# Query and key rows through device memory, value sums two iterations behind, and another order inside the score batches, in a fused attention and feed-forward block

## The chip, the cores and the metric

The kernel runs on one core of a Trainium2 chip. The metric is the device time of one execution in microseconds; lower is better. TensorE (PE) does the matmuls, ScalarE (ACT), VectorE (DVE) and GpSimd (POOL) the work on elements, and the queue of SyncE (SP) issues most transfers; ACT's queue issues some, between its own instructions.

## The reference

A transformer block with adaptive layer norm on S = 2048 tokens of D = 640, one batch, in fp32: 32 heads of 20, a causal window of 256, a feed-forward width of 1536.

```python
mod = (silu(c) @ w_mod).reshape(1, 6, 1, -1)
sa, ca, ga, sb, cb, gb = (mod[:, i] for i in range(6))
h = layernorm(x) * (1 + ca) + sa
q, k, v = (h @ wqkv) as (heads, tokens, 20) each
scores = q @ k.T * 20 ** -0.5
p = softmax(where(0 <= i - j < 256, scores, -1e9))
x = x + ga * ((p @ v) @ wo)
h = layernorm(x) * (1 + cb) + sb
x = x + gb * (gelu(h @ w1 + b1) @ w2 + b2)
```

## The kernel before

Matmuls of fp32 operands are made of three products of a high and a low part each (hi by hi, lo by hi, hi by lo). The program runs in stages: the modulation and the first projections; a loop over attention, into which the other projections are woven; the rest of the attention output and its projection; and the feed-forward part.

**The loop.** The sequence is two halves of 1024 tokens. A quad is four heads, and there are 8 quads in a half; a block is 128 tokens, 8 in a half. An iteration t takes one (half, quad, block), 128 in all. It holds, in this order on PE:

- the scores s of item t (keys by queries, for the row maximum), and the scores e of the item LAG = 11 earlier (for the exponential). s and e are one *score batch*: four heads each, two on the upper and two on the lower rows of the PE array, in two or three PSUM banks. The matmuls of a batch are six kinds: a the upper rows' part in the bank that both row halves share, b and c the upper rows' in their own banks, d and e the lower rows' own, f the lower rows' shared part. The order is the table ONE (one batch) or BOTH (e is batch 0, s batch 1). [...]
- the value sums o of a query block whose last exponential came PVLAG = 1 iteration earlier (pv_stage), which ACT copies to oT (pv_copy) ahead of the exponential of e to pt (e_exp). In between DVE masks e, and POOL cuts a triangle off pt (affine_select).
- the work that a plan has put there for (t, 0..3): projection units of 15 matmuls (pp), layer norm steps, weight loads, modulation.

Every eighth iteration PE transposes the row maxima of the last quad, ACT copies them to mt (m_rows), and four transfers on ACT's queue put them as rows 60, 61, 124 and 125 into that quad's two query buffers (m_store), so that e comes out with the maximum subtracted. e reads them three iterations later.

**Rows.** A unit of q or k makes 128 features of 512 tokens. ACT writes the high part, POOL or DVE the low part into a stage tile, one buffer for q and one for k with both unit halves of 1024 tokens (tags stage0, stage1). When the second is finished (build), its rows are cut by head and put on a list; flush issues from it two to four pieces in an iteration on SP's queue, two transfers each, into the query and key buffers qbuf and kbuf. They hold two heads each (a pair: head e on partitions from 64e, 60 rows: hi, copy of hi, lo), NBUF = 9 of each. The key buffers' last 256 columns of the first half are carried to the second by k_scr in device memory. Until the pieces have landed, ACT may not write the next unit into the stage tile.

**What sets the order.** Each engine's queue runs in order, and the code is recorded in the order in which it stands (Ordered, line 112: the profile names every instruction by that line). UNITS is the order of the units, which a planner places by due times into iterations. Transfers of SP and ACT together take eight semaphores in turn; a transfer waits until the one eight before it has landed, if that is not known already, and an engine that issues it stands meanwhile. The prediction's names: pp is the projection bank, pf its copy by ACT for POOL, stage the stage tile, hhi and hlo the normed input, whi and wlo the weights, wraw a weight as loaded, nm the negative maximum, xt an input tile, o_scr the sums in device memory.

Of the kernel before, what the change touches and what calls it, by code (L numbers as in the profile page):

```python
# [17 lines left out]
P = 128  # L18
# [10 lines left out]
NBUF = 9  # L29
NVB = 5  # L30
LAG = 11
PVLAG = 1
# [22 lines left out]
ONE = "0a 0e 0b 0d 0c 0f".split()  # L55
BOTH = "0a 0e 0b 0d 1a 1e 0c 0f 1d 1b 1c 1f".split()
# [10 lines left out]
FL = 4  # L67
# [50 lines left out]
def block_kernel(ctx: ExitStack, tc: tile.TileContext, x, wqkv, wo, w1, b1, w2, b2, c, crow, wmod, wcol, sel, outT):  # L118
# [12 lines left out]
    k_scr = scratch("k_scr", [NP, 124, 256])  # L131
# [242 lines left out]

    qb_ = [att.tile([P, HALF], F32R, name=f"qbuf{i}") for i in range(NBUF)]
    kb_ = [att.tile([P, 256 + HALF], F32R, name=f"kbuf{i}") for i in range(NBUF)]
# [3 lines left out]
    def ones_k(bufs):  # L380
        for i in bufs:
            for e in range(2):
                nc.sync.dma_start(
                    f32(kb_[i][64 * e + 60 : 64 * e + 64, :]).rearrange("p (r n) -> p r n", n=P),
                    ones[0:4, None, :].to_broadcast([4, (256 + HALF) // P, P]),
                )


    def qbuf(half, pair):
        return qb_[(half * NP + pair) % NBUF]  # L390

    def kbuf(half, pair):
        return kb_[(half * NP + pair) % NBUF]

# [5 lines left out]
    stage = {}  # L400
    quads = {}
    early = [nc.sync]
    clock = [0]
    now = [0]
    pending = []
    done_pairs = set()
    done_v = set()
    last_v = {}
    built = {(0, 0): 4 * DH, (0, 1): 4 * DH}

    def ready(half, pair):
        n = half * NP + pair - NBUF
        return n < 0 or n in done_pairs

    def build(half, kind, j):
        parts = stage.pop((half, kind, j))
        f = j * P
        while f < (j + 1) * P:
            h, d0 = divmod(f, DH)
            n = min(DH - d0, (j + 1) * P - f)  # L420
            if half or h >= 4:
                pending.append((half, kind, h, d0, n, f - j * P, parts, clock[0]))
            f += n

    def flush(limit=2):
        for _ in range(limit):
            able = [p for p in pending if ready(p[0], p[2] // 2) and p[-1] < clock[0]]
            if not able:
                return
            urgent = [p for p in able if 8 * (p[0] * QUADS + p[2] // 4) <= now[0] + 8]  # L430
            piece = urgent[0] if urgent else able[0]
            pending.remove(piece)
            half, kind, h, d0, n, r0, parts, _ = piece
            pair = h // 2
            dst, off = (qbuf(half, pair), 0) if kind == 0 else (kbuf(half, pair), 256)
            if half == 1 and (half, pair) not in built:
                nc.sync.dma_start(f32(kbuf(half, pair)[0:124, 0:256]), k_scr[pair])

            r = 64 * (h % 2)
            src = f32(parts[r0 : r0 + n])  # L440
            two = src if kind == 0 else src[:, 0:1].to_broadcast([n, 2, HALF])
            eng = early[0] if kind else nc.sync
            eng.dma_start(f32(dst[r + 2 * d0 : r + 2 * (d0 + n), off : off + HALF]), two)
            nc.sync.dma_start(f32(dst[r + 40 + d0 : r + 40 + d0 + n, off : off + HALF]), src[:, kind])
            built[half, pair] = built.get((half, pair), 0) + n

    def unit(half, kind, j, c2, eng, acc=None):
# [18 lines left out]
        def qk_hi():  # L466
            if c2 == 0:
                assert not [1 for e in pending if e[1] == kind], key
                stage[key] = prj.tile([P, 2, HALF], F32R, tag=f"stage{kind}", name=f"stage{half}_{kind}_{j}")
            nc.scalar.mul(stage[key][:, 0, cs], box["ps"], sc)  # L470
# [6 lines left out]
        def qk_lo():  # L477
            hi, lo = stage[key][:, 0, cs], stage[key][:, 1, cs]
# [4 lines left out]
            if c2 == 1:  # L483
                build(half, kind, j)
# [103 lines left out]
    def s_batch(it):  # L588
        half, quad, qb, g = it["key"]
        if qb == 0:  # L590
            it["quad"]["nm"] = att.tile([P, 4, NQB], F32, tag="nm", bufs=2, name=f"nm{half}_{quad}")
        t, s = score_banks("s", f"s{half}_{quad}_{qb}")
        c0 = 384 - P * min(g + 1, 3)
        parts = []
        for h in HEADS:
            pair, r = 2 * quad + h // 2, slice(64 * (h % 2), 64 * (h % 2) + 60)
            assert built.get((half, pair)) == 4 * DH, (half, pair, built.get((half, pair)))
# [71 lines left out]
    def e_exp(it, e):  # L669
        half, quad, i = it["key"]  # L670
        pt = att.tile([P, 4, 384], F32, tag="pt", bufs=4, name=f"pt{half}_{quad}_{i}")
# [270 lines left out]
    flat = [prj.tile([P, 2, D], F32, tag=f"stage{i}", name=f"wc{i}") for i in range(2)]  # L942
    flat.append(vcar.rearrange("p q b v -> p (q b v)")[:, 0 : 2 * D].rearrange("p (g d) -> p g d", d=D))
    wc = [[t[:, g] for g in range(2)] for t in flat]
# [11 lines left out]
    for b in range(0, 4, 2):  # L956
        xt = att.tile([P, 2, D], F32, tag="pt", bufs=4, name=f"xs1_{b}")
# [6 lines left out]
    sel_t = kb_[NBUF - 1]  # L964
    sel_raw = att.tile([P, 8 * P], F32, tag="pt", bufs=4, name="sel_raw")
    nc.sync.dma_start(sel_raw, sel)
    ones_k(range(4))
# [80 lines left out]
    first = {}  # L1048

    def lay_out(c2, kind):  # L1050

        if c2 == 0:
            first[kind] = stage[0, kind, 0]
        cs = slice(c2 * CHUNK, (c2 + 1) * CHUNK)
        for pair in range(2):
# [10 lines left out]
            matmul(ps, sel_t[:, at : at + P], first[kind][:, 0, cs], start=True, stop=False)  # L1066
            matmul(ps, sel_t[:, at + P : at + 2 * P], first[kind][:, 1, cs], start=False, stop=True)
# [44 lines left out]
    ones_k(range(4, NBUF - 1))  # L1112
# [10 lines left out]
    plan = {(0, 1): [lambda: lay_out(1, 0)], (0, 2): [lambda: lay_out(1, 1), lambda: ones_k((NBUF - 1,))]}  # L1123
# [57 lines left out]
    for i, key, c2, pieces, ev in where:  # L1181
# [47 lines left out]
    def to_mid():  # L1229
        assert not pending  # L1230
        prj_ctx.close()
        open_mid()
# [43 lines left out]
    for t in range(n + LAG + PVLAG + 4):  # L1276
        clock[0] += 1
# [38 lines left out]
        if ei:  # L1316
            half, quad, i = ei["key"]
            if i == NQB - 1:
                done_pairs.update((half * NP + 2 * quad, half * NP + 2 * quad + 1))
        if si and si["key"][2] == NQB - 1:  # L1320
            half, quad = si["key"][:2]
            if half == 0:
                for pair in (2 * quad, 2 * quad + 1):
                    nc.sync.dma_start(k_scr[pair], f32(kbuf(0, pair)[0:124, HALF : HALF + 256]))
        flush(3 if t < 12 else FL if t > 100 else 3 if len(pending) > 8 else 2)
        if t == 8:
            early[0] = nc.sync
    assert not pending and not plan
# [121 lines left out]
```

## Time and profile before

| | |
|---|---|
| median of the runs | 1078.03 us (1077.12 to 1083.52, 3 runs) |
| profiled execution, its own time | 1079.06 us |
| its span (first to last instruction) | 1077.0 us |
| PE busy | 990.3 us, 92% |
| 0 to 104 us | modulation, first projections, first iterations |
| 104 to 550 us | loop with projections |
| 550 to 675 us | loop and output projection without the projections of q, k, v |
| 675 to 1077 us | feed-forward part |

A row of the timeline gives start, length, engine, operation with output and inputs, their shapes, the number of like instructions drawn together, and in brackets the idle time just before on that engine and what ended it. A row of the waits gives who waited for whom, the sum in us, how many times, and the longest. Rows of windows are explained where they stand.

### The profile page before, as it was taken

To read this page: it belongs to the slowest core of one execution; us is meant where nothing else is said; L and a number is where in the kernel's file an instruction comes from. 1 tells how busy PE (TensorE), PEld (TensorE's weight loads), DVE (VectorE), ACT (ScalarE), POOL (GpSimd) and SP (SyncE) were. 2 spreads that over 40 slices of the span, in tenths; PEclk is the share of its full clock that TensorE was granted. 3 is DMA by queue.
4 is the path that set the end of the run, shared out by engine and by line. 5 is a ranking of instruction groups with operands and counts; after the bars stand their busy time and mean duration, and the time that the engine had idled before them with its cause. 6 is when DMAs were issued, how large, how long until landed. Compare 5 with 4: busy or idle time off the path is not lost.

```text
span 1077.0 us, 20212 instructions
## 1 busy us (share of the span) xinstructions
PE 990.3 (92%) x7712; PEld 773.7 (72%) x7712; DVE 575.0 (53%) x943; ACT 442.0 (41%) x773; POOL 517.2 (48%) x712
## 2 busy tenths in 40 slices
PE   8989989788898998899978877999999999999998
PEld 7767667566666766667656654888888888888886
DVE  5544867576765686666677654344443324333112
ACT  3633445354644444355443444334343333323222
POOL 4334554466764444454444544376556525642221
PEclk7899999899999999899988887899999999999999
DMA  8156566426144645552451212344341334213213
GB/s 281 39 113 164 127 169 160 114 77 189 54 131 115 165 130 159 159 150 56 110 176 41 61 34 79 107 139 147 118 142 52 112 104 139 61 50 119 89 49 110
DMA packets 81037, 123.60 MB, mean 115 GB/s; under 512 B 9022, under 2 KB 46478, under 8 KB 80942
## 3 DMA queue, kind: packets, MB, share of 16 engines
q1 hardware_dynamic: 69870, 111.95, 36.6%
q10 hardware_dynamic: 10368, 8.92, 2.7%
q0 software_dynamic: 704, 1.44, 0.7%
q8 instruction: 62, 1.02, 0.4%
q14 instruction: 33, 0.27, 0.1%
HBM read 69.74 MB, written 22.15 MB: 85 GB/s over the span
## 4 chain that ended last, share of the span: by engine, by line
PE 70%; ACT 7%; DMA 7%; POOL 5%; DVE 5%; SPq 3%; issue 2%; ACTq 1%; POOLq 0%; DVEq 0%
PE h L112 15%; PE out L112 15%; PE pp L112 13%; PE o L112 6%; PE wo L112 6%; PE e L112 5%; PE s L112 4%; ACT pt L112 4%; SPq L112 3%; POOL pt L112 2%; DVE e L112 2%; DMA qbuf<-stage 2%; DMA o_scr<-oT 1%; DMA qbuf<-mt 1%; ACTq L112 1%
## 5 line engine op out<-in xcount | busy, mean ns | idle before, releaser
L112 POOL TENSOR_SCALAR_AFFINE_SELECT pt<-pt 128x512 f32<-128x512 f32 x192 | 129.6, 675 | 176.7 <-ACT pt L112 170.1
L112 DVE TENSOR_REDUCE nm<-s 128x4 f32<-128x1024 f32 (+1 forms) x128 | 152.6, 1192 | 4.4
L112 POOL TENSOR_TENSOR w2lo<-w2r,w2hi 128x640 fp32r<-128x640 f32 x48 | 75.9, 1582 | 153.9 <-ACT w2hi L112 153.7
L112 PE MATMUL e<-qbuf,kbuf 62*128 62x128 f32 (+2 forms) x792 | 113.8, 341 | 32.6 <-ACT pt L112 32.2
L112 PE MATMUL pp<-hhi,whi 128*128 128x512 f32 x275 | 122.7, 446 | 19.7 <-ACT pf L112 16.5
L112 ACT ACTIVATE pt<-e 128x1024 f32<-128x1024 f32 (+1 forms) x120 | 134.0, 1117 | 16.5 <-DVE e L112 15.9
L112 PEld LDWEIGHTS e<-qbuf,kbuf 62*128 62x128 f32 x792 | 80.6, 200 | 75.9 <-ACT pt L112 52.0
L112 ACT COPY oT<-o 128x128 f32<-128x128 f32 x128 | 34.1, 267 | 228.8 <-PE o L112 190.6
L112 PE MATMUL o<-pt,vbuf 128*32 128x128 f32 x2688 | 111.3, 295 | 8.0 <-POOL pt L112 6.2
L112 DVE CAST ghi<-g 128x512 fp32r<-128x512 f32 x48 | 25.0, 522 | 172.8 <-ACT g L112 172.7
L112 DVE COPY_PREDICATED e<-mask_t,e 128x512 f32<-128x512 uint32 x96 | 66.5, 693 | 94.7 <-PE e L112 90.8
L112 PE MATMUL s<-kbuf,qbuf 60*128 60x256 f32 (+2 forms) x744 | 113.7, 323 | 2.9 <-DVE nm L112 2.3
L112 PE MATMUL pp<-hlo,whi 128*128 128x512 f32 x275 | 114.8, 417 | 0.6 <-POOL hlo L112 0.6
L112 PE MATMUL pp<-hhi,wlo 128*128 128x512 f32 x275 | 114.7, 417 | 0.2 <-POOL wlo L112 0.2
L112 POOL TENSOR_TENSOR wlo<-wraw,whi 128x128 fp32r<-128x128 f32 x185 | 80.4, 465 | 40.9 <-ACT whi L112 33.6
L112 PE MATMUL h<-yhi,w1hi 128*128 128x512 f32 x240 | 96.5, 402 | 0.0
L112 PE MATMUL out<-ghi,w2hi 128*128 128x512 f32 x240 | 96.1, 401 | 0.0
L112 PE MATMUL h<-ylo,w1hi 128*128 128x512 f32 x240 | 94.6, 394 | 0.0
L112 PE MATMUL h<-yhi,w1lo 128*128 128x512 f32 x240 | 94.4, 393 | 0.0
L112 PEld LDWEIGHTS o<-pt,vbuf 128*32 128x32 f32 x2688 | 70.9, 116 | 32.5 <-POOL pt L112 11.2
L112 PE MATMUL out<-ghi,w2lo 128*128 128x512 f32 x240 | 93.8, 391 | 0.0
L112 PE MATMUL out<-glo,w2hi 128*128 128x512 f32 x240 | 93.8, 391 | 0.0
(167 smaller groups left out, 1864.5 us busy)
## 6 DMA issues: line engine op xcount, KB each, us to landing
w2r<-in_w SPq DMA_DIRECT2D x48, 320.0 KB
wraw<-in_wqkv SPq DMA_DIRECT2D x38, 320.0 KB
qbuf<-stage SPq DMA_DIRECT2D x52, 160.0 KB
o_scr<-oT ACTq DMA_DIRECT2D x64, 128.0 KB
kbuf<-stage SPq DMA_DIRECT2D x45, 160.0 KB
wm<-in_wmod SPq DMA_DIRECT2D x20, 320.0 KB
ob<-o_scr SPq DMA_DIRECT2D x16, 320.0 KB
xb<-in_x SPq DMA_DIRECT2D x16, 320.0 KB
```

What stands on the lines that cost most here:

```text
L112: return self.tc.keep_in_program_order(op(*args, **kw))
```

## The change

**Rows.** Stage tiles are 512 tokens of one kind, four buffers under one tag. In the iteration after a unit half is finished, rows_out writes it with two transfers of 128 partitions to q_scr or k_scr in device memory (features by hi, hi, lo by tokens). rows_in reads a quad's four heads back with two transfers of 60 partitions for a kind, into buffers that now hold a quad (NSLOT = 4, each as long as two of the old); it is planned READ = 8 iterations ahead of the quad's first, or two iterations behind the last unit that makes its features where that is later. In the second half the key read takes the 256 columns before it along, so the carry is gone. Rows of a head are interleaved (3d, 3d+1, 3d+2). build, flush and their lists are gone.

**Sums.** PVLAG is 2, and pt has five buffers instead of four.

**Maxima.** The first pair of mt's transfers leaves at the end of the iteration in which it left before, the second an iteration later.

**Order.** ONE and BOTH are new: the parts in the shared banks of both batches stand in the first three places. UNITS of the second half have q and k of the first quads ahead of v.

```diff
-NBUF = 9
+NSLOT = 4
-PVLAG = 1
+PVLAG = 2
-    (1, "q00", "k00", "v00", "q01", "k01", "v01", "q1", "k1", "v1", "q2", "k2", "v20", ...
+    (1, "q00", "k00", "q10", "k10", "q01", "k01", "q11", "k11", "v0", "v1", "q2", "k2", ...
-ONE = "0a 0e 0b 0d 0c 0f".split()
-BOTH = "0a 0e 0b 0d 1a 1e 0c 0f 1d 1b 1c 1f".split()
+ONE = "0a 0d 0b 0e 0c 0f".split()
+BOTH = "0a 0d 1a 0b 0e 0c 1d 1c 0f 1b 1f 1e".split()
...
+    def rows_in(half, quad, kind):
+        i = (half * QUADS + quad) % NSLOT
+        src = qk_scr[kind].rearrange("(Q a e d) l s -> Q e (d l) a s", a=2, e=2, d=DH)[quad]
+        to = qb_[i] if kind == 0 else kb_[i] if half else kb_[i][:, :, 256:]
+        c0 = half * (HALF - 256 * kind)
+        for e in range(2):
+            nc.sync.dma_start(f32(to[64 * e : 64 * e + 60]), src[e][:, :, c0 : c0 + to.shape[2]])
...
-    def flush(limit=2):
...
+    def rows_out():
+        due = [w for w in writes if w[-1] < now[0]]
+        for half, kind, j, c2, st, _ in due:
...
+            nc.sync.dma_start(qk_scr[kind][fs, 0:2, ts], two)
+            nc.sync.dma_start(qk_scr[kind][fs, 2, ts], f32(st[:, kind]))
...
         def qk_hi():
-            if c2 == 0:
-                assert not [1 for e in pending if e[1] == kind], key
-                stage[key] = prj.tile([P, 2, HALF], F32R, tag=f"stage{kind}", ...)
-            nc.scalar.mul(stage[key][:, 0, cs], box["ps"], sc)
+            box["st"] = prj.tile([P, 2, CHUNK], F32R, tag="stage", bufs=4, ...)
+            nc.scalar.mul(box["st"][:, 0], box["ps"], sc)
...
         nc.scalar.copy(mt, ps[0:64])
         it["mt"] = mt
-        m_store(it, 0)
...
+    for half in range(2):
...
+        for quad in range(QUADS):
+            if half or quad:
+                js = range(4 * quad * DH // P, (4 * quad * DH + 4 * DH - 1) // P + 1)
+                due = 8 * (half * QUADS + quad)
+                t = due - READ
+                for kind in range(2):
+                    t = max([t, due - 8 * NSLOT + LAG + 8] + [over_at.get((kind, j), -9) + 2 for j in js])
+                    put(max(t, 0), 3, lambda half=half, quad=quad, kind=kind: rows_in(half, quad, kind))
+                    t += 1
...
+        rows_out()
         for h in range(4):
...
+        for a in range(2):
+            if 8 <= t - a <= n and (t - a) % 8 == 0:
+                m_store(s_items[t - a - 1], a)
         for key in pv_at.get(t, ()):
             pv_store(*key)
-        if turn_m:
-            m_store(s_items[t - 1], 1)
...
-        flush(3 if t < 12 else FL if t > 100 else 3 if len(pending) > 8 else 2)
```

PE, an iteration of the second half in which e of quad 2, block 3 (e1_2_3) and s of quad 3, block 6 (s1_3_6) are made, before; qbuf and kbuf are buffers of one pair, o the value sums:

```order
L112 MATMUL e1_2_3_5639<-qbuf3_96,kbuf3_105 128x256
L112 MATMUL e1_2_3_5639<-qbuf2_95,kbuf2_104 128x128
L112 MATMUL e1_2_3_5639<-qbuf3_96,kbuf3_105 128x128
L112 MATMUL e1_2_3_5639<-qbuf3_96,kbuf3_105 128x384
L112 MATMUL s1_3_6_5640<-kbuf5_107,qbuf5_98 128x256
L112 MATMUL s1_3_6_5640<-kbuf4_106,qbuf4_97 128x128
L112 MATMUL e1_2_3_5639<-qbuf2_95,kbuf2_104 128x384
L112 MATMUL e1_2_3_5639<-qbuf2_95,kbuf2_104 128x256
L112 MATMUL s1_3_6_5640<-kbuf5_107,qbuf5_98 128x384
L112 MATMUL s1_3_6_5640<-kbuf5_107,qbuf5_98 128x128
L112 MATMUL s1_3_6_5640<-kbuf4_106,qbuf4_97 128x384
L112 MATMUL o1_2_1_5656<-pt1_2_0_5503,vcar_116 32x128 x4
```

The same iteration now, where a buffer holds a quad:

```order
L112 MATMUL e1_2_3_5476<-qbuf2_95,kbuf2_99 128x256
L112 MATMUL e1_2_3_5476<-qbuf2_95,kbuf2_99 128x384
L112 MATMUL s1_3_6_5477<-kbuf3_100,qbuf3_96 128x256
L112 MATMUL e1_2_3_5476<-qbuf2_95,kbuf2_99 128x128 x2
L112 MATMUL e1_2_3_5476<-qbuf2_95,kbuf2_99 128x384
L112 MATMUL s1_3_6_5477<-kbuf3_100,qbuf3_96 128x384 x2
L112 MATMUL e1_2_3_5476<-qbuf2_95,kbuf2_99 128x256
L112 MATMUL s1_3_6_5477<-kbuf3_100,qbuf3_96 128x128
L112 MATMUL s1_3_6_5477<-kbuf3_100,qbuf3_96 128x256
L112 MATMUL o1_2_0_5493<-pt1_2_0_5360,vcar_106 32x128 x8
```

e's last matmul was the eighth of twelve and is the ninth; s begins third instead of fifth; the sums are those of block 0 (o1_2_0), where block 1 stood.

ACT, the exchange of the maxima of quad 1 in the second half, before; mt is the transposed maxima, oT the copied sums, pt an exponential, and a name in brackets starting with DMAHW is the semaphore of an earlier transfer:

```order
L112 COPY mt1_1_4860<-pm1_1_4858 64x128 [waits PE_49]
L112 DMA qbuf0_93<-mt1_1_4860 2x8x128 [waits DMAHW4_49,Activation_49]
L112 DMA qbuf0_93<-mt1_1_4860 2x8x128 [waits DMAHW6_49]
L112 DMA o_scr<-oT1_0_1_4778 128x256 [waits DMAHW0_49]
L112 DMA qbuf1_94<-mt1_1_4860 2x8x128 [waits DMAHW2_49]
L112 DMA qbuf1_94<-mt1_1_4860 2x8x128 [waits DMAHW4_49]
L112 COPY oT1_0_2_4905<-o1_0_4_4892 128x128 [waits DMAHW5_49,PE_49]
L112 ACTIVATE pt1_0_6_4907<-e1_0_6_4875 128x4x256 [waits DVE_49,Pool_49]
```

And now:

```order
L112 COPY mt1_1_4737<-pm1_1_4735 64x128 [waits DMAHW4_49,DMAHW5_49,DMAHW1_49,PE_49]
L112 DMA qbuf1_94<-mt1_1_4737 2x8x128 [waits DMAHW6_49,Activation_49]
L112 DMA qbuf1_94<-mt1_1_4737 2x8x128 [waits DMAHW0_49]
L112 COPY oT1_0_1_4718<-o1_0_3_4763 128x128 [waits PE_49]
L112 ACTIVATE pt1_0_6_4777<-e1_0_6_4746 128x4x256 [waits DVE_49,Pool_49]
L112 CAST whi103_4791<-wraw103_4609 128x640 [waits DMAHW5_49]
L112 ACTIVATE stage3_1_2_4799<-pp3_1_2_4728 128x512 [waits PE_49]
L112 ACTIVATE pf3_1_2_4801<-pp3_1_2_4728 128x512 [waits Pool_49]
L112 DMA qbuf1_94<-mt1_1_4737 2x8x128 [waits DMAHW2_49]
L112 DMA qbuf1_94<-mt1_1_4737 2x8x128 [waits DMAHW3_49]
```

Before, the fourth transfer waited on DMAHW4, on which the first had waited too; now the second pair leaves behind the next iteration's exponential and copies, and waits for DMAHW2 and DMAHW3.

SP, around the load of the weight wraw113 and the reading of the denominators rd, before:

```order
L112 DMA kbuf4_106<-stage1_1_2_4801 8x1x1024 [waits DMAHW5_49,Activation_49]
L112 DMA kbuf4_106<-stage1_1_2_4801 4x1024 [waits DMAHW6_49,Pool_49]
L112 DMA kbuf4_106<-stage1_1_2_4801 40x1x1024 [waits DMAHW7_49]
L112 DMA kbuf4_106<-stage1_1_2_4801 20x1024 [waits DMAHW0_49]
L112 DMA kbuf5_107<-stage1_1_2_4801 40x1x1024 [waits DMAHW1_49]
L112 DMA kbuf5_107<-stage1_1_2_4801 20x1024 [waits DMAHW2_49]
L112 DMA r_scr<-rd0_4919 32x4x128 [waits DMAHW4_49,DVE_49]
L112 DMA kbuf5_107<-stage1_1_2_4801 40x1x1024 [waits DMAHW5_49]
L112 DMA kbuf5_107<-stage1_1_2_4801 20x1024 [waits DMAHW6_49]
L112 DMA kbuf7_109<-k_scr 124x256 [waits DMAHW7_49,PE_49]
L112 DMA qbuf7_100<-stage1_0_2_4589 40x1x1024 [waits DMAHW0_49,PE_49]
L112 DMA qbuf7_100<-stage1_0_2_4589 20x1024 [waits DMAHW1_49]
```

And now:

```order
L112 DMA k_scr<-stage2_1_2_4681 128x2x512 [waits DMAHW4_49,Activation_49]
L112 DMA k_scr<-stage2_1_2_4681 128x512 [waits DMAHW5_49,Pool_49]
L112 DMA qbuf3_96<-q_scr 60x2x1024 [waits DMAHW7_49,PE_49]
L112 DMA qbuf3_96<-q_scr 60x2x1024 [waits DMAHW1_49,PE_49]
L112 DMA rd0_4789<-o_scr 128x1x128 [waits DMAHW3_49,DMAHW5_49,DMAHW2_49,DMAHW6_49,DMAHW0_49,Activation_49]
L112 DMA k_scr<-stage3_1_2_4799 128x2x512 [waits Activation_49]
L112 DMA k_scr<-stage3_1_2_4799 128x512 [waits DMAHW7_49,Pool_49]
L112 DMA wraw113_4849<-in_wqkv 128x640
L112 DMA wm5_4_4862<-in_wmod 128x640 [waits DMAHW1_49,DVE_49]
L112 DMA r_scr<-rd0_4789 32x4x128 [waits DVE_49]
L112 DMA kbuf3_100<-k_scr 60x2x1280 [waits DMAHW7_49,DMAHW6_49,DMAHW4_49]
L112 DMA kbuf3_100<-k_scr 60x2x1280 [waits DMAHW5_49]
```

In both stretches a key unit's rows leave the stage tile. Before, they went to the key buffers in pieces; now they go to device memory, two transfers a unit half, and the reads of the quad stand between other rows in the queue and wait for the writes.

More of the change, by code (lines that the diff above doesn't have):

```diff
@@ L373, in w_lo @@
         eng.tensor_tensor(lo[:, kt], raw[:, kt], f32(hi[:, kt]), ALU.subtract)
-    qb_ = [att.tile([P, HALF], F32R, name=f"qbuf{i}") for i in range(NBUF)]
-    kb_ = [att.tile([P, 256 + HALF], F32R, name=f"kbuf{i}") for i in range(NBUF)]
+    qb_ = [att.tile([P, 2, HALF], F32R, name=f"qbuf{i}") for i in range(NSLOT)]
+    kb_ = [att.tile([P, 2, 256 + HALF], F32R, name=f"kbuf{i}") for i in range(NSLOT)]
     vq_ = [att.tile([P, NQB, VQ], F32, name=f"vbuf{i}") for i in range(NVB)]
@@ L383, in ones_k @@
                 nc.sync.dma_start(
-                    f32(kb_[i][64 * e + 60 : 64 * e + 64, :]).rearrange("p (r n) -> p r n", n=P),
-                    ones[0:4, None, :].to_broadcast([4, (256 + HALF) // P, P]),
+                    f32(kb_[i][64 * e + 60 : 64 * e + 64]).rearrange("p a (r n) -> p (a r) n", n=P),
+                    ones[0:4, None, :].to_broadcast([4, 2 * (256 + HALF) // P, P]),
                 )
     def qbuf(half, pair):
-        return qb_[(half * NP + pair) % NBUF]
+        return qb_[(half * QUADS + pair // 2) % NSLOT][:, pair % 2]
     def kbuf(half, pair):
-        return kb_[(half * NP + pair) % NBUF]
+        return kb_[(half * QUADS + pair // 2) % NSLOT][:, pair % 2]
+    def rows_in(half, quad, kind):
[5 more added lines that the diff above has]
+            nc.sync.dma_start(f32(to[64 * e : 64 * e + 60]), src[e][:, :, c0 : c0 + to.shape[2]])
+        if kind:
+            there.add((half, quad))
     def vblk(half, quad, kb):
@@ L398, in vblk @@
         return vq_[(half * QUADS + quad) % NVB][:, kb]
-    stage = {}
+    writes, first = [], {}
+    there = {(0, 0)}
     quads = {}
[L402 to L406, printed above, removed]
+    now = [-1]
     done_v = set()
     last_v = {}
[L409 to L423, printed above, removed]
@@ L425, in flush @@
-    def flush(limit=2):
[L426 to L445, printed above, removed]
+    def rows_out():
+        due = [w for w in writes if w[-1] < now[0]]
+        for half, kind, j, c2, st, _ in due:
+            fs, ts = slice(j * P, (j + 1) * P), slice(half * HALF + c2 * CHUNK, half * HALF + (c2 + 1) * CHUNK)
+            two = f32(st) if kind == 0 else f32(st[:, 0:1]).to_broadcast([P, 2, CHUNK])
+            nc.sync.dma_start(qk_scr[kind][fs, 0:2, ts], two)
+            nc.sync.dma_start(qk_scr[kind][fs, 2, ts], f32(st[:, kind]))
+        del writes[: len(due)]
@@ L466, in qk_hi @@
         def qk_hi():
-            if c2 == 0:
-                assert not [1 for e in pending if e[1] == kind], key
-                stage[key] = prj.tile([P, 2, HALF], F32R, tag=f"stage{kind}", name=f"stage{half}_{kind}_{j}")
-            nc.scalar.mul(stage[key][:, 0, cs], box["ps"], sc)
+            box["st"] = prj.tile([P, 2, CHUNK], F32R, tag="stage", bufs=4, name=f"stage{ch}_{kind}_{j}")
+            nc.scalar.mul(box["st"][:, 0], box["ps"], sc)
         def qk_full():
@@ L482, in qk_lo @@
                 eng.tensor_tensor(lo, box["f"], f32(hi), ALU.subtract)
-            if c2 == 1:
-                build(half, kind, j)
+            writes.append((half, kind, j, c2, box["st"], now[0]))
+            if j == 0 and half == 0:
+                first[kind, c2] = box["st"]
         def v_copy():
@@ L596, in s_batch @@
             pair, r = 2 * quad + h // 2, slice(64 * (h % 2), 64 * (h % 2) + 60)
-            assert built.get((half, pair)) == 4 * DH, (half, pair, built.get((half, pair)))
+            assert (half, quad) in there
             k0 = 256 + (qb - 2) * P + c0
@@ L670, in e_exp @@
         half, quad, i = it["key"]
-        pt = att.tile([P, 4, 384], F32, tag="pt", bufs=4, name=f"pt{half}_{quad}_{i}")
+        pt = att.tile([P, 4, 384], F32, tag="pt", bufs=5, name=f"pt{half}_{quad}_{i}")
         for kb, q0, q1, col, n in e_parts(it)[0]:
@@ L940, in block_kernel @@
     nc.scalar.activation(silr, silr, AF.Silu)
-    flat = [prj.tile([P, 2, D], F32, tag=f"stage{i}", name=f"wc{i}") for i in range(2)]
-    flat.append(vcar.rearrange("p q b v -> p (q b v)")[:, 0 : 2 * D].rearrange("p (g d) -> p g d", d=D))
-    wc = [[t[:, g] for g in range(2)] for t in flat]
+    wc = [[prj.tile([P, 2, CHUNK], F32, tag="stage", bufs=4, name=f"wc{j}{g}").rearrange("p a n -> p (a n)")[:, 0:D] for g in range(2)] for j in range(2)]
+    flat = vcar.rearrange("p q b v -> p (q b v)")[:, 0 : 2 * D].rearrange("p (g d) -> p g d", d=D)
+    wc.append([flat[:, g] for g in range(2)])
     wc += [[vq_[i + g].rearrange("p b v -> p (b v)")[:, 0:D] for g in range(2)] for i in (1, 3)]
@@ L962, in block_kernel @@
         wc_load(j)
-    sel_t = kb_[NBUF - 1]
-    sel_raw = att.tile([P, 8 * P], F32, tag="pt", bufs=4, name="sel_raw")
+    sel_t = kb_[NSLOT - 1].rearrange("p a n -> p (a n)")
+    sel_raw = att.tile([P, 8 * P], F32, tag="pt", bufs=5, name="sel_raw")
     nc.sync.dma_start(sel_raw, sel)
-    ones_k(range(4))
+    ones_k(range(NSLOT - 1))
     n0, n1 = {}, {}
@@ L1065, in lay_out @@
             at = ((kind * 2 + pair) * 2) * P
-            matmul(ps, sel_t[:, at : at + P], first[kind][:, 0, cs], start=True, stop=False)
-            matmul(ps, sel_t[:, at + P : at + 2 * P], first[kind][:, 1, cs], start=False, stop=True)
+            matmul(ps, sel_t[:, at : at + P], first[kind, c2][:, 0], start=True, stop=False)
+            matmul(ps, sel_t[:, at + P : at + 2 * P], first[kind, c2][:, 1], start=False, stop=True)
             dst, off = (qbuf(0, pair), 0) if kind == 0 else (kbuf(0, pair), 256)
@@ L1209, in block_kernel @@
             put(t1, 3, *ev)
+    for half in range(2):
+        over_at = {}
+        for _, key, _, pieces, _ in where:
+            if key[0] == half:
+                over_at[key[1:]] = pieces[-1][0]
+        for quad in range(QUADS):
[5 more added lines that the diff above has]
+                    t = max([t, due - 8 * NSLOT + LAG + 8] + [over_at.get((kind, j), -9) + 2 for j in js])
+                    assert t < due - 1, (half, quad, t)
+                    put(max(t, 0), 3, lambda half=half, quad=quad, kind=kind: rows_in(half, quad, kind))
+                    t += 1
     for n, ((g, at), lo) in enumerate(zip(((2, 0), (4, 1), (3, 2), (5, None)), MODS)):
@@ L1229, in to_mid @@
     def to_mid():
-        assert not pending
+        assert not writes
         prj_ctx.close()
@@ L1311, in block_kernel @@
                 go()
+        for a in range(2):
+            if 8 <= t - a <= n and (t - a) % 8 == 0:
+                m_store(s_items[t - a - 1], a)
         for key in pv_at.get(t, ()):
             pv_store(*key)
-        if turn_m:
-            m_store(s_items[t - 1], 1)
[L1316 to L1324, printed above, removed]
-        flush(3 if t < 12 else FL if t > 100 else 3 if len(pending) > 8 else 2)
-        if t == 8:
-            early[0] = nc.sync
-    assert not pending and not plan
+    assert not writes and not plan
     att_ctx.close()
@@ L1437 @@
             for d in range(DH):
-                for low, row in zip(part, (2 * d, 2 * d + 1, 40 + d)):
+                for low, row in zip(part, (3 * d, 3 * d + 1, 3 * d + 2)):
                     pick[kind, h // 2, low, DH * h + d, 64 * (h % 2) + row] = 1.0
```

25 lines of the change are left out of this document (9 added, 16 removed).

## Prediction

> **What bounds the kernel now.** I read the page first, then busy time by stage, then one ordinary iteration of the attention loop, and last every idle stretch of TensorE (PE) over 1 us with what ended it.
>
> ```profile
> span 1077.0 us, 20212 instructions
> PE 990.3 (92%) x7712; PEld 773.7 (72%) x7712; DVE 575.0 (53%) x943; ACT 442.0 (41%) x773; POOL 517.2 (48%) x712
> PEclk7899999899999999899988887899999999999999
> ```
>
> PE is busy 92% of the span, so a gain must come out of its 87 us of idle time, or out of the slices in which the granted clock (last row) is under 9. The stages follow; columns are window, length, busy time of PE, weight loads, DVE, ACT and POOL, then granted clock, DMA share and GB/s.
>
> ```profile
> 104.00:250.00 146.00, 130.36 (x1317) 93.07 (x1316) 103.33 (x139) 69.22 (x129) 80.30 (x125) 0.95 0.48 126
> 250.00:400.00 150.00, 136.12 (x1417) 98.46 (x1416) 104.23 (x140) 71.86 (x136) 81.82 (x135) 0.98 0.48 131
> 400.00:550.00 150.00, 136.31 (x1514) 100.03 (x1511) 102.81 (x131) 70.47 (x131) 74.26 (x108) 0.97 0.49 129
> 550.00:675.00 125.00, 96.94 (x1105) 73.24 (x1105) 72.62 (x121) 52.03 (x90) 57.99 (x85) 0.78 0.23 69
> 675.00:1077.00 402.00, 397.74 (x1922) 335.32 (x1920) 141.17 (x274) 134.83 (x213) 181.55 (x191) 1.00 0.33 103
> ```
>
> From 675 us on (the feed-forward part) PE idles 4 of 402 us at full clock, and no instruction there changes: it costs the same after. All that can move lies in 104 to 675, where PE idles 71 us. An ordinary iteration there, from one score block to the next:
>
> ```profile
> 476.14 0.55 PE L112 MATMUL e<-qbuf,kbuf 62*128 62x256 f32 x4
> 477.13 0.70 DVE L112 COPY_PREDICATED e<-mask_t,e 128x512 f32<-128x512 uint32 x1 [1.45 <-PE e L112]
> 477.24 0.86 PE L112 MATMUL o<-pt,vbuf 128*32 128x128 f32 x24
> 478.17 0.27 ACT L112 COPY oT<-o 128x128 f32<-128x128 f32 x1 [1.32 <-PE o L112]
> 478.34 1.03 ACT L112 ACTIVATE pt<-e 128x1024 f32<-128x1024 f32 x1
> 480.54 0.55 PE L112 MATMUL e<-qbuf,kbuf 62*128 62x256 f32 x4
> ```
>
> The chain is score block (476.14 to 477.24, 1.10 us), value sums o (0.86), copy oT, exponential (until 479.37): 3.23 us of an iteration of 4.40, the rest of which PE fills with projections. So an ordinary iteration is bound by PE, and a stall of another engine is paid in full where it outlasts that filling.
>
> **The change part by part.**
>
> *Rows through device memory.* The idle stretches that the row moves cause: the waits view has PE waiting 16.5 us in 9 places for the ACT copy pf that frees the projection bank; the four largest follow, with ACT's side and SyncE's (SP) queue ahead of the longest, and the window around each.
>
> ```profile
> PE pp L112 <- ACT pf L112: 16.5, 9, 7.0
> 148.06 0.50 PE L112 MATMUL pp<-hhi,whi 128*128 128x512 f32 x1 [2.46 <-ACT pf L112]
> 208.29 0.80 PE L112 MATMUL pp<-hhi,whi 128*128 128x512 f32 x1 [6.96 <-ACT pf L112]
> 336.27 0.50 PE L112 MATMUL pp<-hhi,whi 128*128 128x512 f32 x1 [2.31 <-ACT pf L112]
> 437.83 0.50 PE L112 MATMUL pp<-hhi,whi 128*128 128x512 f32 x1 [2.45 <-ACT pf L112]
> 207.15 0.60 ACT L112 ACTIVATE stage<-pp 128x512 fp32r<-128x512 f32 x1 [7.35 <-DMA wraw<-in_wqkv]
> 193.75 9.38 SPq L112 DMA_DIRECT2D kbuf<-stage  x8
> 144.00:155.00 11.00, 8.54 (x79) 6.19 (x79) 4.83 (x7) 4.08 (x7) 3.67 (x7) 0.84 0.47 126
> 199.00:215.00 16.00, 8.36 (x75) 6.08 (x75) 5.52 (x12) 2.77 (x6) 5.71 (x11) 0.68 0.43 106
> 331.00:341.00 10.00, 7.27 (x57) 4.98 (x55) 4.06 (x6) 3.63 (x6) 4.62 (x7) 0.83 0.61 137
> 433.00:447.00 14.00, 11.52 (x96) 8.58 (x96) 8.14 (x13) 3.97 (x7) 6.58 (x10) 0.76 0.67 189
> ```
>
> ACT may not overwrite the one stage buffer of a kind until its row moves, up to eight in SP's queue, have landed; the releaser named, a weight load, stands between them in that queue. A clock of c over a window of w us is 2(1-c)w us at half clock, and each costs half of itself: (0.16x11)+(0.17x10)+(0.24x14) = 6.8 us, and at 199 to 215, where some 3.4 of its 10.2 slow us lie in the gap itself, another 3.4. With 14.2 us for the four gaps (the other five waits, 2.3 us, are left to stay) that is 24.4. A stage buffer will hold one unit half, four stand in turn, and each is free after two writes: I take **-24**, ends -14 (gaps alone) and -27 (all of the waits).
>
> That short gaps bring the half clock is read from the rows: 2.46 us in 144 to 155 with 3.5 us at half. [...]
>
> *Running maximum's second pair.* Every 8 iterations ACT issues four small transfers mt; in three places the second pair waited for the first to land, ACT stood, and PE behind it:
>
> ```profile
> 411.36 2.51 ACTq L112 DMA_DIRECT2D qbuf<-mt  x2
> 413.96 0.27 ACT L112 COPY oT<-o 128x128 f32<-128x128 f32 x1 [6.47 <-DMA o_scr<-oT]
> 415.21 0.55 PE L112 MATMUL e<-qbuf,kbuf 62*128 62x128 f32 x5 [3.83 <-ACT pt L112]
> 521.98 0.33 PE L112 MATMUL e<-qbuf,kbuf 62*128 62x128 f32 x2 [2.22 <-ACT pt L112]
> 555.22 0.44 PE L112 MATMUL pv<-idn,vT 128*128 128x128 f32 x2 [3.09 <-ACT oT L112]
> 408.00:421.00 13.00, 9.17 (x93) 6.69 (x94) 6.30 (x8) 5.03 (x8) 4.98 (x10) 0.87 0.52 145
> 550.00:577.00 27.00, 18.79 (x201) 14.74 (x202) 15.35 (x19) 8.91 (x17) 8.26 (x10) 0.62 0.40 131
> ```
>
> Gaps 9.1, slow clock 1.7 at the first, none at the second, and at the third between 0 and 10.3 (20.5 slow us, of which I give this stall some 8, so 4): **-15**, ends -9 and -21. In the new order of ACT the pairs stand an iteration apart, and the second waits for other transfers than the first.
>
> In return that pair is late, and its rows are read three iterations after the maximum. The exchange after the ordinary iteration:
>
> ```profile
> 485.99 1.28 ACTq L112 DMA_DIRECT2D qbuf<-mt  x2
> 488.39 0.79 ACT L112 COPY vbuf<-pv 128x64 f32<-128x64 f32 x4
> 493.14 0.61 PE L112 MATMUL e<-qbuf,kbuf 62*128 62x256 f32 x5
> ```
>
> The pair would now leave behind the copy that ends at 489.18, its second transfer about 489.8, and be read at 493.14: 3.3 us to land. The trace shows no landing of it alone; the pair at 411.36 could be issued once the first, issued at 407.52, had landed, so 3.84 us is the most in a crowded queue, which would be 0.5 late, 16 times 8 us, or 35 with half a slow window (1.7) each. At the other end it is in time. I take **+5**, ends 0 and +35.
>
> *Sums two iterations behind, and waits beside.*
>
> ```profile
> PE o L112 <- POOL pt L112: 6.2, 10, 1.9
> 260.88 0.55 PE L112 MATMUL e<-qbuf,kbuf 62*128 62x256 f32 x4 [2.52 <-ACT pt L112]
> 251.49 2.77 SPq L112 DMA_DIRECT2D xt<-in_x  x4
> ```
>
> The sums wait 6.2 us for POOL's triangle cut of the last exponential. An iteration (4.40) more covers the longest, 1.87 us: **-5**, ends -6 and 0. The fifth pt buffer keeps the exponential from waiting for its tile. The units of the second half come in another order, q and k ahead of v, with as many matmuls, copies and weight loads as before: 0, as PE's filling hides where they stand. The loop runs one iteration longer; its drain adds between nothing, where projections of the output fill it, and one chain of 3.23: **+1.5**. The gap at 260.88 follows input tiles issued at 251.49, behind row moves in SP's queue: **-3**, ends -4 and 0.
>
> *Score order.* Of the block's twelve matmuls the last one for e was the eighth and is the ninth, so e ends one matmul (1.10/12 = 0.09 us) later. Behind it stands the mask, which ended at 477.83 while the exponential began at 478.34 behind oT: 0.5 us cover the 0.09. Some 117 iterations have both batches; where the cover is gone, +11. Three neighbours of one row half instead of four could also save as much as one matmul. I take **+3**, ends -11 and +11.
>
> *What the rows cost now.* In the program order SP falls from 582 to 418 transfers, POOL's ten go, ACT's 128 stay: 80 writes and 60 reads stand for what the next two rows count (with 32 carries of keys and ten rows of ones).
>
> ```profile
> L112 SPq DMA_DIRECT2D qbuf<-stage x136: 563/746/3317, 51.0 to 531.4; - x136
> L112 SPq DMA_DIRECT2D kbuf<-stage x126: 557/744/1377, 59.4 to 545.7; - x126
> ```
>
> At 0.74 us each about 120 us of issue leave SP, but the bytes cross twice; the DMA share stood at 0.48 and I leave it there. A quad's reads are due 8 iterations (35 us) ahead, except where the units end late: the keys of the last quads of the second half are read 3 iterations ahead (13 us), first read behind a weight load. Estimate **+2** for one such quad late (a gap of 2.3 us, as above), ends 0 and +10. Reads wait for the landing of writes and hold what stands behind them in SP's queue; for weights so delayed **+3**, ends 0 and +30 (below).
>
> Sum: -24-15-5-3 = -47; +5+1.5+3+2+3 = +14.5; -32.5. The profiled execution took 1079.06 us (span 1077.0 and 2.1 around it), 1.0 above the median of 1078.03: 1079.1-32.5 = 1046.6, less the 1.0: **about 1046**.
>
> **The rivals.**
>
> *The late pair decides (slower).* If the second mt pair takes 4.9 us to land, e of each of the 16 quads begins 1.6 us late and, with a slow window, loses 3.3: 53 us, so 1046-5+53 = **1094**. It outweighs the gain from 4.6 us of landing on, when it costs 3.0 each (1089). For it speaks that ACT's queue will have writes and reads of 0.3 to 0.6 MB running beside it; against it, the 3.84 us above as the most.
>
> *SP's queue stalls anew (within 1%).* The reads' waits stand in front of weight loads and stage writes; of 15 quads with two reads each, if every fourth of the 30 costs a gap with its slow clock as the short ones above (about 4 us), that is +30: **1073**, in the band 1067 to 1089. The gap of 7 us at 208.29 was made in just this way. [...] The reads' distance of 35 us speaks against it.
>
> *The clock stays up (faster still).* 550 to 675 ran at 0.78: 55 us at half clock. If the longer distance of the sums also closes the small gaps there and half of it goes, 14 us more: **1032**. Against it: the chain of 3.23 us remains there without projections to fill it.
>
> *The score order costs its full 11 instead of 3*: **1054**; the change of rows does not do what it says (buffers freed no sooner): -24 and -3 fall away, which also ends at **1073** and shares the second rival's chance.
>
> **How the numbers follow.** Forecast 0.57, its own range 1030 to 1062 (terms' ends of one size up or down, not all at once); late pair 0.12; stalls anew 0.16; clock up 0.08; score order 0.07. About 1% (1067 and 1089) is what a measurement can tell from no change. Faster: 0.57+0.08+0.07 and 0.04 of the stalls that fall short of it, 0.76; within: the other 0.12 of the stalls and 0.01 of the late pair, 0.13; slower 0.11. Leaving out 0.05 below and 0.15 above, the range is **1024 to 1073**.
>
> **What would show it.** Right: no ACT wait of the stage copies for a transfer over 1 us, PE's 16.5 us for pf down to 3 or less, no wait of sums for POOL, oT's waits for mt and o_scr transfers gone, clock 0.98 and above in 104 to 550. Wrong: waits of e for qbuf's mt transfers after each exchange (late pair); pp or whi waiting for wraw or reads from device memory (stalls anew); a score block longer than 1.10 us, with exponentials released by the mask. The forecast as a whole is wrong if PE's idle time in 104 to 675 does not fall from 71 us to about 45.

## The result

The changed kernel takes 1092.77 us (median of 4 runs, 1091.07 to 1094.34) against 1077.96 before: a ratio of 1.0126, 95% interval 1.0089 to 1.0163. It is slower by about 14 us, where 1046 was forecast. The profiled execution took 1094.34 us, its span 1092.3. Ratios leave out the few runs more than 1.5% above the fastest of their kernel, medians are of all runs.

From the page of the changed kernel: span, busy time, granted clock and DMA share by slices, and the queue that SP fills.

```profile
span 1092.3 us, 19853 instructions
PE 986.5 (90%) x7712; PEld 776.2 (71%) x7712; DVE 579.0 (53%) x943; ACT 444.2 (41%) x773; POOL 510.9 (47%) x702
PEclk8899899999899999989976968899999999999999
DMA  8357658726548717871573111424442244213313
q1 hardware_dynamic: 80932, 142.71, 43.7%
```

The last two rows before the change:

```profile
DMA  8156566426144645552451212344341334213213
q1 hardware_dynamic: 69870, 111.95, 36.6%
```

PE does the same work in 4 us less, yet the span is 15 us longer: 19 us more idle time. The DMA row has slices of 7 and 8 in the first half, where mostly 4 to 6 stood before. By stages (columns as in the prediction):

```profile
104.00:250.00 146.00, 124.54 (x1250) 90.81 (x1249) 100.47 (x134) 66.77 (x123) 77.56 (x120) 0.94 0.62 185
250.00:400.00 150.00, 129.27 (x1366) 94.49 (x1367) 97.05 (x133) 69.94 (x131) 76.17 (x130) 0.95 0.60 171
400.00:550.00 150.00, 135.67 (x1495) 101.11 (x1486) 101.28 (x129) 68.52 (x124) 73.95 (x108) 0.97 0.58 171
550.00:675.00 125.00, 98.65 (x1080) 77.25 (x1079) 75.90 (x119) 52.03 (x91) 59.64 (x84) 0.77 0.36 97
```

In 104 to 550 PE idles 56.5 us (43.2 before), and the DMA engines stand at 0.60 (0.48 before). In 104 to 675 it idles 83 us (71 before), where the forecast had about 45. The waits of the changed kernel (who waits for whom: us, times, longest):

```profile
PE e L112 <- DMA qbuf<-mt: 37.0, 14, 4.4
PE s L112 <- DVE nm L112: 12.1, 23, 1.3
ACT oT L112 <- DMA qbuf<-mt: 6.5, 3, 2.8
PE s L112 <- DMA kbuf<-k_scr: 6.6, 3, 3.4
ACT oT L112 <- DMA o_scr<-oT: 4.4, 2, 3.1
PE pp L112 <- ACT pf L112: 0.6, 1, 0.6
```

The rows of ACT and of s before:

```profile
ACT oT L112 <- DMA o_scr<-oT: 21.8, 6, 6.5
ACT oT L112 <- DMA qbuf<-mt: 11.4, 3, 4.9
PE s L112 <- DVE nm L112: 2.3, 4, 0.7
```

The last row of the changed kernel is what was to vanish, and it has: 16.5 us before, 0.6 now. Of PE's waits of o for POOL's cut (6.2 before) no row is left. In their place stand 37.0 us in which e waits for the maxima, which did not exist before. One exchange in the timeline: ACT's queue, SP's queue, and PE.

```profile
200.35 1.28 ACTq L112 DMA_DIRECT2D qbuf<-mt  x2
202.88 1.57 SPq L112 DMA_DIRECT2D qbuf<-q_scr  x2
204.19 0.62 ACTq L112 DMA_DIRECT2D qbuf<-mt  x1
205.28 0.89 SPq L112 DMA_DIRECT2D kbuf<-k_scr  x2
207.55 0.62 ACTq L112 DMA_DIRECT2D qbuf<-mt  x1
212.21 0.38 PE L112 MATMUL e<-qbuf,kbuf 62*128 62x256 f32 x1 [2.85 <-DMA qbuf<-mt]
216.41 0.69 PE L112 MATMUL e<-qbuf,kbuf 62*128 62x384 f32 x1 [3.83 <-DMA qbuf<-mt]
203.00:218.00 15.00, 7.03 (x56) 5.12 (x55) 6.11 (x12) 3.94 (x6) 5.66 (x11) 0.84 0.98 262
```

Between the first pair of maxima and the last transfer of the second SP issues a quad's reads of q (0.96 MB) and k (0.96 MB). The DMA engines are then busy 98% of 15 us (the window's row), and the second pair, 8 KB a transfer, issued at 204.19 and 207.55, lets e go on only at 212.21 and 216.41, 8.0 and 8.9 us later. PE does 7.0 us of work in these 15. The chain of the work that ended last (start, length, what) shows a second way in which the bulk traffic holds the pair:

```profile
201.97 5.56 DMA wraw<-in_wqkv
207.55 8.81 DMA qbuf<-mt
```

By this chain the last transfer of the pair was issued only when a weight load that SP had issued at 201.97 had landed, 5.56 us later, and so 3.4 us behind the first: SP's and ACT's transfers take the same eight semaphores in turn. READ = 8 is the reason that they meet: a quad's reads start 8 iterations ahead of its first, so in the iteration of the exchange (q) and in the next (k), in which the second pair leaves.

### The profile page after: what moved, and what is told of

Its sections match the earlier page's. It is cut to its first block, busy times and chain, and to the rows that moved or that the text cites. A ratio compares the mean times of both kernels' runs of the same rounds, so it can differ in the third digit from the quotient of the medians.

```text
span 1092.3 us, 19853 instructions
## 1 busy us (share of the span) xinstructions
PE 986.5 (90%) x7712; PEld 776.2 (71%) x7712; DVE 579.0 (53%) x943; ACT 444.2 (41%) x773; POOL 510.9 (47%) x702
## 3 DMA queue, kind: packets, MB, share of 16 engines
q1 hardware_dynamic: 80932, 142.71, 43.7%
## 4 chain that ended last, share of the span: by engine, by line
PE 63%; DMA 15%; DVE 8%; POOL 5%; ACT 4%; issue 3%; SPq 1%; ACTq 0%; POOLq 0%; DVEq 0%
PE h L112 15%; PE out L112 15%; PE pp L112 10%; DMA qbuf<-mt 6%; PE wo L112 6%; PE o L112 5%; PE e L112 5%; PE s L112 4%; ACT pt L112 3%; DVE nm L112 2%; DVE e L112 2%; DMA kbuf<-k_scr 2%; DMA wraw<-in_wqkv 1%; DVE s L112 1%; POOL wlo L112 1%
## 5 line engine op out<-in xcount | busy, mean ns | idle before, releaser
L112 PE MATMUL e<-qbuf,kbuf 62*128 62x128 f32 (+2 forms) x792 | 128.2, 342 | 58.2 <-DMA qbuf<-mt 37.0
L112 PEld LDWEIGHTS e<-qbuf,kbuf 62*128 62x128 f32 x792 | 89.3, 205 | 102.3 <-ACT pt L112 43.2
L112 PE MATMUL s<-kbuf,qbuf 60*128 60x256 f32 (+2 forms) x744 | 118.9, 315 | 19.3 <-DVE nm L112 12.1
L112 PEld LDWEIGHTS s<-kbuf,qbuf 60*128 60x128 f32 x744 | 99.0, 200 | 36.4 <-issue 10.3
```

Of the source, the lines that this page charges most:

```text
L112: return self.tc.keep_in_program_order(op(*args, **kw))
```

## The experiments

All ratios are to the kernel before, on the same chip, with 95% intervals.

**Both pairs in the exchange iteration.**

```diff
-        for a in range(2):
-            if 8 <= t - a <= n and (t - a) % 8 == 0:
-                m_store(s_items[t - a - 1], a)
+        if turn_m:
+            for a in range(2):
+                m_store(s_items[t - 1], a)
```

> The changed kernel, with both pairs of the maxima's transfers at the end of the exchange iteration (the second an iteration earlier than in the changed kernel). Theory 1, late pair behind the quad's reads: PE's waits of e for these transfers fall from 37.0 us in 14 places to under 8, with the slow clock after them another 15 to 20 go, about 1045 to 1055 us. Rival, score order: the waits fall but others take their place, above 1080. Rival, the queue of ACT: the pairs wait for each other again as before the change (oT for mt or o_scr some 15 us), 1060 to 1070.

Measured: 1068.54 us, 0.9911 (0.9879 to 0.9943). Its waits:

```profile
ACT oT L112 <- DMA qbuf<-mt: 41.4, 12, 5.7
PE e L112 <- ACT pt L112: 32.2, 32, 2.9
PE s L112 <- DMA kbuf<-k_scr: 5.5, 2, 3.5
```

PE's direct waits for the maxima are gone, but the time is 13.5 us above theory 1's range and in that of the rival of ACT's queue: the slow transfers now hold ACT for 41.4 us, since the pairs stand closer together in its queue again. Much of that PE seems to fill with projections, as its waits of e for pt are 32.2 us, no more than before the change. So the transfers are slow whether or not e is the one to wait for them, which lateness alone does not explain.

**Reads moved, pair left late.**

```diff
-READ = 8
+READ = 12
```

> The changed kernel with READ = 12 in place of 8: reads of a quad leave up to four iterations earlier, so not in the two iterations in which the maxima's pairs leave. Theory 1a, the pair is slow because the reads (480 and 600 KB each) stand in front of it in the DMA engines: waits of e for the pair fall from 37.0 to under 12, about 1055 to 1068 us, although the pair leaves as late as now. Theory 1b, lateness alone: the waits stay at 30 or more and the time within 8 us of 1092.

Measured: 1062.25 us, 0.985 (0.9804 to 0.9897), 30 us faster than the changed kernel by one number that moves no work. Its waits and the same window as above:

```profile
PE e L112 <- DMA qbuf<-mt: 4.9, 5, 1.7
PE s L112 <- DVE nm L112: 12.8, 25, 1.3
PE s L112 <- DMA kbuf<-k_scr: 5.5, 3, 3.2
203.00:218.00 15.00, 13.70 (x148) 10.04 (x144) 12.88 (x21) 9.50 (x17) 9.90 (x19) 1.00 0.57 189
```

37.0 us of waits become 4.9 with the pair at the same place in ACT's program. A weight load and a unit's writes still leave in this window (SP issues them from 201.80 to 206.55); the quad's reads left at 185.63 and 192.48. So the cause is the meeting with the reads, not the lateness alone.

**The old score tables.** ONE and BOTH as before the change, in the changed kernel.

> The changed kernel with the score tables ONE and BOTH of before. Theory 1 (pair and reads): waits of e for the pair stay between 30 and 40, the time falls by 0 to 12 us, what s waits for the negative maximum (12.1 us on PE against 2.3 before the change). Rival, the order is the main cost: over 25 us faster, below 1067.

Measured: 1093.71 us, 1.011 (1.0075 to 1.0145) against 1.0126. The waits of e for the pair stay, at 39.5 us (in a profiled execution of 1100 us). The order is not the cause.

**The late pair in the kernel before.**

```diff
         it["mt"] = mt
-        m_store(it, 0)
...
         for key in pv_at.get(t, ()):
             pv_store(*key)
-        if turn_m:
-            m_store(s_items[t - 1], 1)
+        for a in range(2):
+            if 8 <= t - a <= n and (t - a) % 8 == 0:
+                m_store(s_items[t - a - 1], a)
```

The pairs leave behind the store of the sums (pv_store) here, and ahead of it in the changed kernel.

> The kernel before, with the maxima's transfers as in the change alone: the first pair at the end of the exchange iteration, the second an iteration later. Theory 1a (reads in front): no bulk reads here, the pair lands in 2 to 4 us, waits of e under 8 us, and the ACT stands on the first pair's landing (15 us) go: 1065 to 1082. Theory 1b (lateness alone): waits of e of 25 us or more, 1095 to 1115.

Measured: 1063.35 us, 0.9866 (0.9819 to 0.9913), and once more beside later runs:

> The kernel before with the late pair alone again, on the same chip as the other two, to compare with them: 1063, within 3 us.

1064.78 us, 0.9876 (0.9833 to 0.9919). This small part alone gains 14 to 16 us, about what the whole change lost. The waits of the first of the two runs:

```profile
PE e L112 <- DMA qbuf<-mt: 4.1, 5, 1.7
PE pp L112 <- ACT pf L112: 9.6, 5, 5.5
PE o L112 <- POOL pt L112: 5.5, 10, 1.9
ACT oT L112 <- DMA o_scr<-oT: 1.6, 1, 1.6
```

The first is 2 us under the range of theory 1a, far from 1b's. Without bulk reads the late pair is in time, and ACT's stands go (for o_scr 21.8 us before, 1.6 now; for mt 11.4 before, no row now). The second row says more: PE's waits for pf fell from 16.5 to 9.6 us with the row moves untouched. Of the four gaps over 2 us that they had, two are left (5.5 and 3.2 us), and the gap of 2.52 us at 260.88, which the prediction also gave to the row moves, is gone.

**The order, with the reads out of the way** (READ = 12 and the old tables):

> The changed kernel with READ = 12 and the score tables of before. With the reads out of the way the order alone is seen. If the order is worth its shorter block (1.00 against 1.11 us, 117 times 0.11 = 13 us) this is 8 to 13 us slower than with READ = 12 alone (1062), about 1070 to 1075. If what s waits for the negative maximum (12.8 us there) takes it back, within 4 us of 1062.

Measured: 1066.35 us, 0.9846 (0.98 to 0.9892) against 0.985 with the new tables. And the new tables on the kernel before with the late pair:

> The kernel before with the late pair and the new score tables, nothing of the rows or the sums. If the order gains its 13 us where no bulk reads run: 1050 to 1055. If it is a wash: 1060 to 1066, with s waiting for the negative maximum 10 us or more on PE.

1066.09 us, 0.9861 (0.9813 to 0.9909) against 0.9866, with 8.5 us of waits of s for the maximum in place of the 10 expected (4.1 with the old tables). Three pairs of kernels differ by 0.2% or less: a wash. A block that nothing holds did become shorter. One of the changed kernel, whose six e and six s end where the sums begin:

```profile
299.92 0.44 PE L112 MATMUL e<-qbuf,kbuf 62*128 62x256 f32 x2
300.55 0.44 PE L112 MATMUL s<-kbuf,qbuf 60*128 60x384 f32 x4
300.92 0.43 PE L112 MATMUL o<-pt,vbuf 128*32 128x128 f32 x8
```

1.00 us in place of 1.10. But s now starts third and waits for the maximum of the item before: 2.3 us before, 12.1 in the changed kernel, and with READ = 12 and the old tables

```profile
PE s L112 <- DVE nm L112: 8.0, 14, 1.1
```

against 12.8 with the new ones. These 4.8 us are less than half of the expected gain of 13, so they do not take it back alone. But most of that gain never came: about 80 blocks of each trace have all six e and six s with the sums right behind them, and from their first matmul to the first of the sums these take, together, 103.8 us with the new tables and 105.9 with the old (READ = 12), and 102.1 against 100.6 in the kernel before with the late pair. What lengthens the other blocks, beside the waits for the maximum, stays open.

**One iteration less for the sums** (READ = 12, PVLAG = 1, four pt buffers):

> The changed kernel with READ = 12, PVLAG = 1 and four pt buffers. Theory, the sums' second iteration is worth the 5 us that I summed: sums wait some 6 us for POOL, about 1065 to 1069. Rival, worth nothing, since the waits' slack is taken elsewhere and the drain is an iteration shorter: 1058 to 1063.

Measured: 1067.91 us, 0.988 (0.9843 to 0.9917) against 0.985. The waits of o for POOL are back:

```profile
PE o L112 <- POOL pt L112: 6.1, 8, 2.0
```

The medians are 5.7 us apart, as summed, the ratios only 0.003 (3 us), and the intervals overlap: it is worth between nothing and some 6 us. PVLAG = 2 on the old row moves wasn't tried.

**Reads spaced by hand.**

```diff
-                t = due - READ
+                t = due - (6 if half and quad == QUADS - 1 else 12 if due > 24 else READ)
...
-                    put(max(t, 0), 3, lambda ...: rows_in(half, quad, kind))
+                    if t > due - 5:
+                        for part in range(2):
+                            put(t + 2 * part, 3, lambda ...: rows_in(half, quad, kind, part))
+                    else:
+                        put(max(t, 0), 3, lambda ...: rows_in(half, quad, kind))
```

rows_in then moves all columns, or (part 0, part 1) all but the last 512 and these. due is 8 times the quad's number from zero, so due > 24 holds from the fifth quad on; the fourth still has 8.

> The changed kernel with the reads spaced by hand: 12 iterations ahead from the fourth quad on, 8 for the first ones (early weights behind them cost 9 us with READ = 12 everywhere), 6 for the last quad of the second half, and a read that comes less than five iterations ahead split by columns, the first blocks' part first. If reads in the wrong place are what is left over in the changed kernel: keys late at iterations 64 and 112 (11 us with READ = 12) and the early weights (9 us) go, 1040 to 1050. If not: within 4 us of 1062.

Measured: 1063.07 us (1049.67 to 1065.86), 0.9793 (0.9719 to 0.9867). That is 13 us above the first range and within the second. The waits for keys (0.4 us) and early weights (1.9) are all but gone, but with 8 iterations for the first quads those met the pair again: 14.3 us of waits of e, 8.6 of them in the first two exchanges. So the next one gave the third quad 6 iterations and the fourth 12:

```diff
-                t = due - (6 if half and quad == QUADS - 1 else 12 if due > 24 else READ)
+                t = due - (6 if due == 16 or half and quad == QUADS - 1 else 12)
```

> As the kernel with spaced reads, but the third quad's read 6 iterations ahead (behind the pair of iterations 8 and 9, in whose way it stood, 8.6 us of waits in iterations 11 and 19) and the fourth quad's 12. If placing is what counts: those waits go, 1048 to 1056. If it is noise of the transfers: within 4 us of 1062.

Measured: 1058.57 us (1047.49 to 1063.0), 0.9803 (0.9758 to 0.9848): the fastest kernel by its median, 34 us below the changed one. Its median is 2.6 us above the expected range and falls into the one for noise (within 4 us of 1062). Its interval overlaps those of READ = 12 alone and of the first spacing, so a gain of the spacing over READ = 12 is not shown. The waits of its profiled execution, the fastest of its six (1047.49):

```profile
PE e L112 <- DMA qbuf<-mt: 7.6, 6, 3.0
PE s L112 <- DVE nm L112: 12.0, 23, 1.3
PE pp L112 <- ACT pf L112: 0.9, 3, 0.6
PE s L112 <- DMA kbuf<-k_scr: 0.8, 1, 0.8
```

**The rows alone**, spaced like this, with the late pair, PVLAG = 1, four pt buffers and the old tables (the order of the units is the new one):

> The rows through device memory alone, reads spaced in the same way, and the late pair: PVLAG = 1, four pt buffers, the score tables of before. Beside the kernel before with the late pair (1063) this tells what the rows are worth. By my sum -24 + 5 = -19: 1044. If the stage waits were mostly the same waits that the pair's move takes away: -9 to +5, 1054 to 1068.

Measured: 1059.93 us, 0.9817 (0.9784 to 0.985) against 0.9876 (0.9833 to 0.9919) without the rows on the same chip: some 5 us, with intervals that just overlap, and not 19. But the collision is not out of it. The waits of e and pp with the rows, and then without them:

```profile
PE e L112 <- DMA qbuf<-mt: 15.1, 9, 3.7
PE pp L112 <- ACT pf L112: 0.5, 1, 0.5
PE e L112 <- DMA qbuf<-mt: 5.1, 4, 2.1
PE pp L112 <- ACT pf L112: 9.7, 5, 5.1
```

The 9.2 us less that pp waits for pf stand against 10.0 more that e waits for the maxima. What the rows are worth with every read out of the pair's way, no run shows.

## Why the prediction was wrong

**Where it failed: the late pair, "+5, ends 0 and +35".** PE's waits for it measured 37.0 us, above the upper end, which had the slow clock in it. In time, READ = 12 alone takes back 30 of the 47 us between the forecast and the measurement. What failed in it is the bound: 3.84 us, read from a queue of many small row moves, was taken as the most that a crowded queue does. Its own trace has more: the last transfer of the exchange at 519 us was issued at 519.8 and moved its packets from 523.3 to 524.5, until 4.7 us after its issue. Above all it was an answer about the old traffic. The change replaced that traffic by blocks of 1 MB, and put them into just the iteration in which the pair leaves: READ = 8 and an exchange every 8 iterations. Both numbers stood in the change, and the prediction never set them beside each other.

The rival "the late pair decides" named the mechanism, its place and its time, 1094, with a chance of 0.12. That the time fits within 2 us is in part luck: it is 53 us on a base of 1041 that has the rows at -24, while the runs show 30 to 34 us on a base of 1059 to 1062. It had 4.9 us to land for all 16 quads; in truth some took 8 to 9 us and others were in time. Its objection, that 3.84 us is the most, was the same wrong bound.

**DMA share "stood at 0.48 and I leave it there":** wrong. It is 0.60 in 104 to 550, since the rows cross twice: 142.71 MB on SP's queue against 111.95.

**Rows, "-24":** the waits went as forecast (16.5 to 0.6 us), but the gain in time isn't settled: 5 us over the late pair alone, with 10 us more of waits for the maxima in the way. Part of the term was counted twice: the late pair alone takes the waits for pf from 16.5 to 9.6. The likely reason is that ACT, which frees the stage tiles and the bank, no longer stands in its own queue; no run separates it. Two terms of 24 and 15 us that share an engine's queue were added as if they were apart. The new waits (keys 6.6 us) came on top.

**The pair's stands, "-15":** right in size, 14 and 16 us in the kernel before with the late pair alone (1065 and 1063 against 1079), as long as no bulk reads stand in its way. The parts are others, so the fit is in part luck: the gaps at 415.21 and 521.98 are gone, in place of the one at 555.22 stands one of 3.0 us at 545.82, and the rest came from the waits for pf.

**Sums, "-5":** the waits went from 6.2 us to none; the time agrees in size but isn't resolved. **Input tiles, "-3":** the gap is gone, but also in the kernel before with the late pair, whose row moves are the old ones; so the row moves are not shown to be its cause. **The drain, "+1.5",** has no run of its own. **Score order, "+3":** a wash within about 4 us; a block that nothing holds was 0.1 us shorter and not as long as before, while the waits of s for the maximum, which the term did not have, rose by 10 us. **Late quads, "+2":** 6.6 us of waits for keys, at the first and the seventh quad of the second half, of which the term had only the later one; inside its bounds. **Weights behind reads, "+3":** not seen as waits of PE in the changed kernel; with READ = 12 everywhere 5.1 us of PE's waits for weights at the start.

The other rivals didn't come: no copy of a weight or of a stage tile holds PE as at 208.29 before, and the clock in 550 to 675 stays at 0.77 (0.78 before).

With the reads spaced, the whole change comes to 1058.6, inside what the forecast called its own range (1030 to 1062) and near its upper end, with 7.6 us of waits for the pair left even in its fastest execution. As a forecast of the change without the collision it was 12 us too low, of the change itself 47.

## What to carry to other kernels

The small transfers on the critical path had no fixed duration here: from issue to first packet those of the second pair took 1.3 us where no read of a quad was issued within 6 us of their exchange, and 1.7 to 6.4 in the others. When a change turns many small transfers into few large ones, price the small ones anew, by setting the issue times of both side by side, iteration by iteration, and look for equal periods. Two stalls of one engine's queue are not added before asking what the first one's cure does to the second.

## What the runs showed of the hardware

Bulk transfers on SP's queue, the reads above all, delayed small ones on ACT's: e waited 37.0 us for the maxima with READ = 8, and 4.9 with READ = 12. In 206 to 214 us of the changed kernel, by the DMA view (packets, MB and share of 16 engines for SP's queue q1 and ACT's q10):

```profile
DMA packets 524, 1.79 MB, mean 224 GB/s; under 512 B 52, under 2 KB 77, under 8 KB 523
q1 hardware_dynamic: 495, 1.76, 95.5%
q10 hardware_dynamic: 28, 0.02, 1.0%
```

495 packets took 95.5% of 16 engines for 8 us, 0.25 us each; ACT's queue got 1.0%, though the transfer issued at 204.19 had not landed and another was issued at 207.55. In 206 to 209 us the only queue with packets is SP's:

```profile
q1 hardware_dynamic: 196, 0.68, 93.7%
```

The 16 packets of 512 B of the transfer issued at 204.19 begin to move at 209.7, 5.5 us after the issue, those of the one issued at 207.55 at 214.0, 6.4 us after. Five of the 16 exchanges have no read of a quad issued within 6 us of them (from 314.7, 386.3, 494.4, 604.8 and 644.9): there the packets of both transfers of the second pair begin 1.3 us after the issue. In the other eleven it is 1.7 to 6.4 us. By what rule the DMA engines divide their time between the two queues, no run shows.
